# Mixing the values of batches 2 and 3 on two row halves of TensorE in four bursts, and a later place for one unit pair

## The chip, the cores and the metric

One core of one Trainium2 chip. The metric is the device time of a run in microseconds. The kernel before takes 250.5 us, so 2%, the limit of "faster", is 5 us.

## The reference, cut to what matters

```python
# attention: 4 batches, 8 heads, 768 positions, 64 per head; 8 blocks of 96
k_sorted = np.einsum('bhij,bhjcd->bhicd', P, k_b)      # P: 8x8 mixing matrix per head
v_sorted = np.einsum('bhij,bhjcd->bhicd', P, v_b)      # <- the changed part, for b = 2, 3
scores = scale * np.matmul(q_b, k_sb.transpose(0, 1, 2, 4, 3))
attn = softmax(scores)
x = np.matmul(attn, v_sb)                              # then to 3072 tokens x 512
# feed-forward
g = x @ w_gate; val = x @ w_val
out = (g / (1 + exp(-g)) * val) @ w_out
```

## The kernel before: the parts concerned

The feed-forward runs in eight passes of 384 tokens (`ffn(0)` to `ffn(7)`). A pass has twelve gate and twelve value groups of four matmuls and three output groups of twelve. Attention work for later passes is merged in between: each side item has a time, and is emitted after the first feed-forward item at whose end the running sum of costs has reached it. TensorE runs the items in the order emitted. A unit is the attention of two heads over four blocks of a batch: eight score matmuls, their exponentials, eight matmuls of probabilities and values, a normalisation on VectorE and, in this pass, four transposes. A burst is what the mixing emits at one place. Matmuls write to banks of PSUM, the memory that other engines then read or copy out.

```python
def v_pair_chunk(pair, at, n, eng, tag):        # mixes v of batches 2 and 3: all 128 rows
    dst = vt_tile(pair).rearrange("p u n e -> p (u n) e")
    mix = rmix["p"].rearrange("p u a b -> p (u a b)")      # 128 x 128, block diagonal
    tp = chunk_tile("tv", n // 4, tag).rearrange("p (l n) -> p l n", n=2 * H * NB)
    for ld in range(n):
        col = (at + ld) * C
        nc.tensor.matmul(tp[:, ld, :], lhsT=vch[:, col:col + 128], rhs=mix, start=True, stop=True)
    drain(eng, dst[:, :, at:at + n], tp[0:C].transpose([0, 2, 1]))   # copy out of PSUM
# ... cut ...
# gate -> tanh on ScalarE -> product gs on VectorE; value -> product h on VectorE.
# gate, value and (partly) output share three PSUM banks, tag "gen".
merge(ffn(1), ... + units(1, range(4), (11.3, 15.8)))
merge(ffn(3), vs(v_pair_chunk, 8, [1.15 * n for n in range(8)]) + units(2, range(4), (9.8, 14.0)))
```

Rows 0 to 63 of the values are batch 2, rows 64 to 127 batch 3, so half of the 128 x 128 mixing matrix is zeros. Mixing and scores share two double banks, tags "a" and "b".

The softmax here doesn't subtract the row's maximum and nothing guards it: scores larger than these inputs give would overflow.

Of the kernel before, what the change touches and what calls it, by code (L numbers as in the profile page):

```python
# [17 lines left out]
def kernel(  # L18
# [11 lines left out]
    nc = tc.nc  # L30

    B, H, S, D = q.shape
    NB = sort_net.shape[-1]
    C = S // NB
# [40 lines left out]
    vch = const.tile([128, D * C + 32], BF16)  # L75
# [51 lines left out]
    lowr, highr = slice(0, R), slice(R, 2 * R)  # L127
# [26 lines left out]
    rmix = {b: const.tile([128, 2, H, NB], BF16, name=f"rmix{b}") for b in (0, 1, "p")}  # L154
# [5 lines left out]
    def vt_tile(pair):  # L160
        if pair not in vts:
            t = vtp.tile([C, 2, H * NB, D + 1], BF16, name=f"vt{pair}", tag="vt")
            nc.vector.memset(t[:, :, :, D:D + 1].rearrange("p u n e -> p (u n) e"), 1.0)
            vts[pair] = t
        return vts[pair]
# [10 lines left out]
    def pair_tile(name, tag):  # L176
        return psum.tile([128, 1024], FP32, name=name, tag=tag)

    def bank_tile(name, tag="gen"):
        return psum.tile([128, 512], FP32, name=name, tag=tag, bufs=3 if tag == "gen" else 1)  # L180
# [28 lines left out]
    def drain(eng, dst, src):  # L209
        if eng == "v":  # L210
            nc.vector.tensor_copy(dst, src)  # L211
        else:
            nc.scalar.copy(dst, src)  # L213
# [10 lines left out]
    def chunk_tile(name, n, tag):  # L224
        return pair_tile(name, tag) if n == 2 else bank_tile(name, tag)
# [21 lines left out]
        drain(eng, dst[:, :, at:at + n], tp[0:C].transpose([0, 2, 1]))  # L247

    def v_pair_chunk(pair, at, n, eng, tag):
        dst = vt_tile(pair).rearrange("p u n e -> p (u n) e")  # L250
        mix = rmix["p"].rearrange("p u a b -> p (u a b)")
        tp = chunk_tile("tv", n // 4, tag).rearrange("p (l n) -> p l n", n=2 * H * NB)
        for ld in range(n):
            col = (at + ld) * C
            nc.tensor.matmul(tp[:, ld, :], lhsT=vch[:, col:col + 128], rhs=mix,  # L255
                             start=True, stop=True)
        drain(eng, dst[:, :, at:at + n], tp[0:C].transpose([0, 2, 1]))

    es, sts, xts = {}, {}, {}
    ecount = [0]  # L260
# [1 line left out]
    def scores(b, u, tag):  # L262
        half, g = divmod(u, H2)
        k_sb, k_at, q_sb, q_at = ((kqts[b], 0, kqts[b], GI * C) if b < 2 else
                                  (kqts["p"], (b - 2) * GI * C, kqts["q"], (b - 2) * GI * C))
        if tag == "gen":
            wide = None
            pss = [bank_tile("qk"), bank_tile("qk")]
        else:
            wide = pair_tile("qk", tag).rearrange("p (two n) -> p two n", two=2)  # L270
            pss = [wide[:, 0], wide[:, 1]]
        for i4 in range(4):
            at = (g * NB + half * 4 + i4) * C
            for two in range(2):
                lo = two * D
                nc.tensor.matmul(pss[two][:, i4 * C:(i4 + 1) * C],  # L276
                                 lhsT=k_sb[lo:lo + D, k_at + at:k_at + at + 128],
                                 rhs=q_sb[lo:lo + D, q_at + at:q_at + at + C],
                                 start=True, stop=True)
        return wide, pss  # L280

    def exps(b, u, wide, pss):
        n = ecount[0] % 8
        ecount[0] += 2
        if wide is None:
            for two in range(2):
                nc.scalar.activation(e_all[:, n + two, 0:4 * C], pss[two][0:C, 0:4 * C], AF.Exp, scale=scale)
        else:
            nc.scalar.activation(e_all[:, n:n + 2, 0:4 * C], wide[0:C, :, 0:4 * C], AF.Exp, scale=scale)  # L289
        es[(b, u)] = [e_all[:, n, :], e_all[:, n + 1, :]]  # L290

    def qk(b, u, tag="b"):
        exps(b, u, *scores(b, u, tag))
# [19 lines left out]
    def xt_tile(tag, n):  # L313
        bank = psum.tile([128, 1024], BF16, name="x_ps", tag=tag, bufs=3 if tag == "gen" else 1)
        return bank[:, 0:n * 4 * C].rearrange("p (g a b) -> p g a b", g=n, b=C)

    def x_to(dst, b, u):
        st = sts.pop((b, u))
        for i4 in range(4):
            nc.tensor.transpose(dst[:, i4, :], st[:, i4].rearrange("p a b -> p (a b)"),  # L320
                                ident[0:C, 0:C])

    def xtr(b, u):
        half, g = divmod(u, H2)
        if g == 0:
            xts[(b, half)] = xtp.tile([128, H2, TW], BF16, name=f"xt{b}_{half}", tag="xt")
        x_ps = xt_tile("x", 1)[:, 0]
        x_to(x_ps, b, u)
        return xts[(b, half)][:, g, :], x_ps.rearrange("p a b -> p (a b)")

    def x_dma(b, u):
        half, g = divmod(u, H2)
        if g == 0:
            xts[(b, half)] = xtp.tile([128, H2, TW], BF16, name=f"xt{b}_{half}", tag="xt")
        nc.sync.dma_start_transpose(out=xts[(b, half)][:, g, :].rearrange("p (i c) -> p i c", c=C),
                                    in_=sts.pop((b, u)).rearrange("p i two d -> p (i two d)"))
# [5 lines left out]
    def q_dma(b):  # L342
        dst = kqt_tile("q")[:, (b - 2) * GI * C:(b - 1) * GI * C]
        nc.sync.dma_start_transpose(out=dst.rearrange("p (g s) -> p g s", g=H2), in_=q_scr[b - 2])
# [5 lines left out]
    def gate(n, m):  # L350
        xt = xts[divmod(n, 2)]
        g_ps = psum.tile([128, TW], FP32, name="g_ps", tag="gen", bufs=3)
        for kc in range(NKC):
            nc.tensor.matmul(g_ps, lhsT=wg_sb[:, kc, ts(m, 128)], rhs=xt[:, kc, :],  # L354
                             start=(kc == 0), stop=(kc == NKC - 1))
        gate_out(n, m, g_ps)
# [66 lines left out]
    for it, n in ((1, 3), (2, 4), (3, 4), (4, 4)):  # L423
        nc.tensor.matmul(idle_ps[0:NB, 0:NB], lhsT=rowreds[it][:, :, 0], rhs=rowreds[it][:, :, 0],
                         start=True, stop=True)
# [38 lines left out]
    for b in range(1, B):  # L464
        rows = highr if b % 2 else lowr
# [49 lines left out]
    man = tc.manual_schedule(engines={ET.PE, ET.Pool})  # L515
    man.__enter__()

    def units(b, us, ats):
        us = list(us)
        todo = []  # L520
        for n, at in enumerate(ats):
            u, u2 = us[2 * n:2 * n + 2]
            held = []
            todo.append((at, lambda u=u, u2=u2, held=held: (qk(b, u, "b"), held.append(scores(b, u2, "a")))))
            todo.append((at + 1.3, lambda u2=u2, held=held: exps(b, u2, *held[0])))
            for w, tag, t in ((u, "b", 1.9), (u2, "a", 3.6)):
                if b == 0 or b == 1 and u < H2:
                    todo.append((at + t, lambda w=w, tag=tag: av(b, w, tag)))
                    todo.append((at + t + 3.1, lambda w=w: drain("v", *xtr(b, w))))
                else:  # L530
                    todo.append((at + t, lambda w=w, tag=tag: (av(b, w, tag), x_dma(b, w))))
        return todo

    def kqs(b, ats):
        return [(at, lambda n=n: (kq_chunk(b, n * 32, 16, "v", "b"), kq_chunk(b, n * 32 + 16, 16, "s", "a")))
                for n, at in enumerate(ats)]

    def vs(f, size, ats):
        return [(at, lambda m=m: f(1, m * size, size, "sv"[m % 2], "ba"[m % 2])) for m, at in enumerate(ats)]

    def merge(main, side):
        done, k = 0.0, 0
        side = sorted(side, key=lambda t: t[0])
        for c, f in main:
            f()
            done += c
            while k < len(side) and side[k][0] <= done:
                side[k][1]()
                k += 1
        while k < len(side):  # L550
            side[k][1]()
            k += 1

    def ffn(n):
        todo = []
        for m in range(NFC):
            if n > 0 or m > 1:
                todo.append((0.65, lambda m=m: gate(n, m)))
            if n > 0 or m > 0:
                todo.append((0.65, lambda m=m: value(n, m)))  # L560
            ends = (6, 9, 11) if n == 1 else (3, 7, 11)
            if n > 0 and m in ends:
                for part in range(3):
                    todo.append((0.87, lambda t3=ends.index(m), part=part: outp(n - 1, t3, part)))
        return todo
# [7 lines left out]
    q_cast(3)  # L573
    both = slice(0, 128)
    merge(ffn(0), units(0, range(4, 8), (0.0, 5.6)))
    merge(ffn(1), vs(v_chunk, 16, (3.2, 3.9, 4.7, 5.5)) + kqs(1, (6.2, 8.2, 10.3)) + units(1, range(4), (11.3, 15.8)))
    for s in range(4):
        copy_v(nc.gpsimd, 1, both, s)
    nc.vector.memset(kqt_tile("p")[:, 2 * GI * C:], 0.0)
    merge(ffn(2), units(1, range(4, 8), (0.0, 5.5)) + kqs("p", (13.0, 16.2, 19.4))  # L580
          + [(13.0, lambda: q_dma(2)), (16.4, lambda: q_dma(3))])
    merge(ffn(3), vs(v_pair_chunk, 8, [1.15 * n for n in range(8)]) + units(2, range(4), (9.8, 14.0)))
    merge(ffn(4), units(2, range(4, 8), (0.0, 8.0)))
    merge(ffn(5), units(3, range(4), (0.0, 8.0)))
    merge(ffn(6), units(3, range(4, 8), (0.0, 8.0)))
# [36 lines left out]
```

## Time and profile before

| | before |
|---|---|
| time, median (4 runs) | 250.51 us (249.94 to 250.79) |
| TensorE busy | 240.2 us, 97% of the span |
| VectorE, ScalarE busy | 157.4 us (63%), 110.3 us (44%) |
| TensorE's share of the chain that ends last | 88% |

The busy shares name TensorE, and the chain of waits confirms it. For a change this small the useful reading is finer: measure from start to start. I use the first scores near 62 us, those near 78 us, the first gate of the fourth pass near 107 us and the first scores of batch 2 near 121 us. In the timeline of TensorE before (columns: start, duration, group; in brackets, where there is one, the idle time before it and what ended that), the two of these that the prediction below does not show are:

```profile
62.20 0.52 PE L276 MATMUL qk<-kqt 64*128 64x96 bf16 x16
...
121.06 0.52 PE L276 MATMUL qk<-kqtq,kqtp 64*128 64x96 bf16 x16
```

So the second pass's stretch is 78.36 - 62.20 = 16.16 us (16.17 from the unrounded starts) and the fourth's is 121.06 - 107.00 = 14.06 us.

### The profile page before, as it was taken

The numbers are of one execution on the slowest core, as the hardware profiler recorded it, in microseconds if no ns is written. First come the engines' busy times: TensorE is split into PE (matmuls) and PEld (weight loads), VectorE is DVE, ScalarE is ACT, GpSimd is POOL, SyncE is SP. The second block draws the span as 40 slices with busy tenths as digits, with TensorE's granted clock in tenths as the row PEclk, the third lists the DMA queues.
The fourth block names the chain that finished last, engine by engine and source line by source line (L and its number), as shares of the span: only waits on it lengthen the run. The fifth ranks groups of instructions, "written<-read, shape, count | busy, mean of one in ns | idle before, by whom it ended". The sixth has DMA issues, their size and how long they took to land.

```text
span 248.1 us, 6062 instructions
## 1 busy us (share of the span) xinstructions
PE 240.2 (97%) x2572; PEld 142.9 (58%) x2572; DVE 157.4 (63%) x332; ACT 110.3 (44%) x187; POOL 52.6 (21%) x47
## 2 busy tenths in 40 slices
PE   7799999999999999999999999999999999999994
PEld 5385566665555556666655655555555555555543
DVE  6677689886555775857657647755764585446700
ACT  3977543453544444455642552354244334232311
POOL 7948449980039400000000000000000000000000
PEclk9999999999999999999999999999999999999999
DMA  5949999999999488010122121112111111100122
GB/s 97 215 83 162 208 198 223 190 219 222 219 175 188 74 195 179 3 42 3 42 53 56 52 67 32 44 45 74 36 42 42 40 55 55 45 19 24 45 81 88
DMA packets 39530, 24.38 MB, mean 98 GB/s; under 512 B 27728, under 2 KB 35664, under 8 KB 38992
## 3 DMA queue, kind: packets, MB, share of 16 engines
q0 software_dynamic: 21328, 14.16, 39.0%
q1 hardware_dynamic: 18176, 9.84, 14.3%
q8 instruction: 20, 0.33, 0.5%
q14 instruction: 6, 0.05, 0.1%
HBM read 28.32 MB, written 7.86 MB: 146 GB/s over the span
## 4 chain that ended last, share of the span: by engine, by line
PE 88%; DVE 4%; ACT 3%; issue 2%; DMA 2%; DVEq 0%; ACTq 0%; POOLq 0%
PE v_ps L372 24%; PE g_ps L354 23%; PE o_ps L389 23%; PE tkq L233 4%; PE av_ps L303 3%; PE qk L276 3%; DMA v<-in_v_dram 2%; PE idle_ps L415 2%; PE tv L245 2%; PE tv L255 1%; DVE gs_sb L364 1%; PE o_ps L405 1%; DVE st L309 1%; PE x_ps L320 1%; DVE h L377 1%
## 5 line engine op out<-in xcount | busy, mean ns | idle before, releaser
L364 DVE SCALAR_TENSOR_TENSOR gs_sb<-th_sb,g_ps 128x384 bf16<-128x384 bf16 x96 | 52.8, 550 | 53.8 <-ACT th_sb L362 51.2
L372 PE MATMUL v_ps<-xt,wv_sb 128*128 128x384 bf16 x380 | 77.3, 326 | 0.3
L354 PE MATMUL g_ps<-xt,wg_sb 128*128 128x384 bf16 x376 | 76.5, 325 | 0.0
L362 ACT ACTIVATE th_sb<-g_ps 128x384 bf16<-128x384 f32 x96 | 47.1, 491 | 57.6 <-PE g_ps L354 55.2
L389 PE MATMUL o_ps<-wo_sb,h 128*128 128x512 bf16 x276 | 64.3, 379 | 0.0
L377 DVE SCALAR_TENSOR_TENSOR h<-v_ps,gs_sb 128x384 bf16<-128x384 f32 x96 | 53.3, 555 | 6.4
L372 PEld LDWEIGHTS <-wv_sb 128*128 128x128 bf16 x380 | 35.6, 97 | 23.9 <-issue 1.2
L354 PEld LDWEIGHTS <-wg_sb 128*128 128x128 bf16 x376 | 34.5, 97 | 22.9 <-issue 0.2
L389 PEld LDWEIGHTS <-h 128*128 128x128 bf16 x276 | 26.3, 98 | 28.3
L394 ACT COPY o_sb<-o_ps 128x512 f32<-128x512 f32 x23 | 13.5, 586 | 49.1 <-PE o_ps L389 46.4
L124 POOL COPY vch<-v 64x1536 bf16<-64x1536 bf16 (+2 forms) x11 | 28.8, 2648 | 20.6 <-PE av_ps L303 17.2
L289 ACT ACTIVATE e_all<-qk 96x768 bf16<-96x768 f32 x30 | 22.6, 802 | 7.7 <-PE qk L276 7.6
L309 DVE TENSOR_TENSOR st<-av_ps,r_sb 96x512 bf16<-96x512 f32 x32 | 21.7, 679 | 0.2
L303 PEld LDWEIGHTS <-e_all 96*128 96x128 bf16 x256 | 12.2, 98 | 5.0 <-ACT e_all L289 0.8
L303 PE MATMUL av_ps<-vt,e_all 96*128 96x65 bf16 x256 | 13.5, 194 | 0.0
L307 DVE RECIPROCAL r_sb<-av_ps 96x8 f32<-96x8 f32 x32 | 6.4, 199 | 8.7 <-PE av_ps L303 8.6
L213 ACT CAST vt<-tv 96x1024 bf16<-96x1024 f32 (+1 forms) x9 | 9.2, 1030 | 4.0 <-PE tv L255 2.6
L211 DVE CAST vt<-tv 96x1024 bf16<-96x1024 f32 (+1 forms) x9 | 9.8, 1100 | 1.2 <-PE tv L245 1.2
L211 DVE CAST kqt<-tkq 128x1024 bf16<-128x1024 f32 (+1 forms) x7 | 7.4, 1068 | 2.5 <-PE tkq L233 2.4
L213 ACT CAST kqt<-tkq 128x1024 bf16<-128x1024 f32 (+1 forms) x7 | 6.0, 894 | 6.4 <-PE tkq L233 6.4
L415 PE MATMUL idle_ps<-warm_sb 128*128 128x512 bf16 x28 | 8.3, 388 | 0.0
L233 PE MATMUL tkq<-rmix,kq 128*64 128x64 bf16 x384 | 7.8, 197 | 0.4 <-issue 0.4
(74 smaller groups left out, 130.5 us busy)
## 6 DMA issues: line engine op xcount, KB each, us to landing
out_dram<-o_sb SPq DMA_DIRECT2D x23, 256.0 KB, 2.0
v<-in_v_dram POOLq DMA_DIRECT2D x3, 768.0 KB, 19.7
kq<-in_q_dram POOLq DMA_DIRECT2D x2, 768.0 KB, 14.1
wg_sb<-in_moe_w_gate_dram POOLq DMA_DIRECT2D x6, 256.0 KB, 9.4
wv_sb<-in_moe_w_val_dram POOLq DMA_DIRECT2D x6, 256.0 KB, 9.8
wo_sb<-in_moe_w_out_dram POOLq DMA_DIRECT2D x1, 1536.0 KB, 24.5
kp<-in_k_dram POOLq DMA_DIRECT2D x2, 768.0 KB, 15.1
q_scr<-in_q_dram POOLq DMA_DIRECT2D x2, 768.0 KB, 30.0
```

Source lines behind the costliest of these rows:

```text
L124: eng.tensor_copy(dst, src.transpose([0, 2, 1]))
L211: nc.vector.tensor_copy(dst, src)
L233: nc.tensor.matmul(tp[two * D:(two + 1) * D, lc, :], lhsT=kq_tiles[b][:, at + lc, :], rhs=rm[:, two], start=True, stop=True)
L289: nc.scalar.activation(e_all[:, n:n + 2, 0:4 * C], wide[0:C, :, 0:4 * C], AF.Exp, scale=scale)
L303: nc.tensor.matmul(o[:, two, i4, :], lhsT=e[:, i4 * C:i4 * C + 128], rhs=vt[:, 2 * g + two, half * 4 + i4, :], start=True, stop=True)
L309: nc.vector.tensor_tensor(st.rearrange("p i two d -> p two i d"), o[0:C, :, :, 0:D], r_sb.to_broadcast([C, 2, 4, D]), op=ALU.mult)
L354: nc.tensor.matmul(g_ps, lhsT=wg_sb[:, kc, ts(m, 128)], rhs=xt[:, kc, :], start=(kc == 0), stop=(kc == NKC - 1))
L362: nc.scalar.activation(th_sb, g_ps, AF.Tanh, scale=0.5)
L364: nc.vector.scalar_tensor_tensor(gs_sb, th_sb, 1.0, g_ps, op0=ALU.add, op1=ALU.mult)
L372: nc.tensor.matmul(v_ps, lhsT=wv_sb[:, kc, ts(m, 128)], rhs=xt[:, kc, :], start=(kc == 0), stop=(kc == NKC - 1))
L377: nc.vector.scalar_tensor_tensor(h_tiles[n][:, m, :], v_ps, 0.5, gs_tiles.pop(m), op0=ALU.mult, op1=ALU.mult)
L389: nc.tensor.matmul(o_ps, lhsT=h_w[:, m, ts(t3, 128)], rhs=wo_sb[:, m, :], start=(m == 0), stop=(m == NFC - 1))
```

## The change

The intent: a 64-row matmul needs only half of TensorE's rows, so the two batches can be mixed side by side, each with 64 columns in place of 128 that are half zeros. The pairs come in four bursts in place of eight, each with one copy for VectorE and one for ScalarE. Separately, the second unit pair of the second pass is put 0.6 further in.

```diff
     def v_pair_chunk(pair, at, n, eng, tag):
-        dst = vt_tile(pair).rearrange("p u n e -> p (u n) e")
-        mix = rmix["p"].rearrange("p u a b -> p (u a b)")
-        tp = chunk_tile("tv", n // 4, tag).rearrange("p (l n) -> p l n", n=2 * H * NB)
+        dst = vt_tile(pair)[:, :, :, at:at + n]
+        tp = chunk_tile("tv", n // 4, tag).rearrange("p (u l n) -> p u l n", u=2, n=H * NB)
         for ld in range(n):
             col = (at + ld) * C
-            nc.tensor.matmul(tp[:, ld, :], lhsT=vch[:, col:col + 128], rhs=mix,
-                             start=True, stop=True)
-        drain(eng, dst[:, :, at:at + n], tp[0:C].transpose([0, 2, 1]))
+            for u, rows in enumerate((lowr, highr)):
+                nc.tensor.matmul(tp[:, u, ld, :], lhsT=vch[rows, col:col + 128],
+                                 rhs=rmix["p"][rows, u].rearrange("p a b -> p (a b)"),
+                                 start=True, stop=True)
+        drain(eng, dst, tp[0:C].transpose([0, 1, 3, 2]))
 # ... cut: units() takes a lag per unit pair, 3.1 where it was fixed ...
+    def v_pairs(ats):
+        return [(at, lambda m=m: (v_pair_chunk(1, m * 16, 8, "v", "b"), v_pair_chunk(1, m * 16 + 8, 8, "s", "a")))
+                for m, at in enumerate(ats)]
 # ... cut ...
-    merge(ffn(1), ... + units(1, range(4), (11.3, 15.8)))
+    merge(ffn(1), ... + units(1, range(4), (11.3, 16.4), (3.1, 2.5)))
-    merge(ffn(3), vs(v_pair_chunk, 8, [1.15 * n for n in range(8)]) + units(2, range(4), (9.8, 14.0)))
+    merge(ffn(3), v_pairs([2.6 * n for n in range(4)]) + units(2, range(4), (9.8, 14.0)))
```

More of the change, by code (lines that the diff above doesn't have):

```diff
@@ L516, with units @@
     man.__enter__()
-    def units(b, us, ats):
+    def units(b, us, ats, lags=(3.1, 3.1)):
         us = list(us)
@@ L522, in units @@
             u, u2 = us[2 * n:2 * n + 2]
+            lag = lags[n]
             held = []
@@ L528, in units @@
                     todo.append((at + t, lambda w=w, tag=tag: av(b, w, tag)))
-                    todo.append((at + t + 3.1, lambda w=w: drain("v", *xtr(b, w))))
+                    todo.append((at + t + lag, lambda w=w: drain("v", *xtr(b, w))))
                 else:
@@ L575 @@
     merge(ffn(0), units(0, range(4, 8), (0.0, 5.6)))
-    merge(ffn(1), vs(v_chunk, 16, (3.2, 3.9, 4.7, 5.5)) + kqs(1, (6.2, 8.2, 10.3)) + units(1, range(4), (11.3, 15.8)))
+    merge(ffn(1), vs(v_chunk, 16, (3.2, 3.9, 4.7, 5.5)) + kqs(1, (6.2, 8.2, 10.3))
+          + units(1, range(4), (11.3, 16.4), (3.1, 2.5)))
     for s in range(4):
```

## The prediction

> **What bounds the kernel now.** I read the page first, then the list of waits, then the timeline of TensorE around the changed code, then those of VectorE and ScalarE in the same stretch. The page's busy line, its TensorE slices and its chain:
>
> ```profile
> PE 240.2 (97%) x2572; PEld 142.9 (58%) x2572; DVE 157.4 (63%) x332; ACT 110.3 (44%) x187; POOL 52.6 (21%) x47
> PE   7799999999999999999999999999999999999994
> PE 88%; DVE 4%; ACT 3%; issue 2%; DMA 2%; DVEq 0%; ACTq 0%; POOLq 0%
> ```
>
> TensorE is full in all slices but the first two and the last, and holds 88% of the chain that ends last. So time saved on TensorE between 24 and 240 us should reach the end one for one, and time that another engine costs counts only where TensorE must wait for it. The list of waits says how much of that there is:
>
> ```profile
> ACT th_sb L362 <- PE g_ps L354: 55.2, 62, 1.3
> DVE gs_sb L364 <- ACT th_sb L362: 51.2, 31, 2.8
> ...
> PE qk L276 <- DVE st L309: 0.6, 1, 0.6
> ```
>
> The long waits are all of other engines for TensorE. After the start, TensorE has one recorded wait of its own: 0.6 us, once. Now the code of the change. The timeline of TensorE, columns start, duration, group:
>
> ```profile
> 107.00 0.81 PE L354 MATMUL g_ps<-xt,wg_sb 128*128 128x384 bf16 x4
> 107.65 0.61 PE L255 MATMUL tv<-rmixp,vch 128*128 128x128 bf16 x8
> 108.10 0.81 PE L372 MATMUL v_ps<-xt,wv_sb 128*128 128x384 bf16 x4
> 108.75 0.61 PE L255 MATMUL tv<-rmixp,vch 128*128 128x128 bf16 x8
> 109.19 0.81 PE L354 MATMUL g_ps<-xt,wg_sb 128*128 128x384 bf16 x4
> ```
>
> From start to start a gate or value group of four takes 0.65 us and a mixing burst of eight takes 0.445 us, 55.6 ns a matmul. Nothing waits; all eight bursts, up to 118.57, go like this. The second place, in the second pass:
>
> ```profile
> 67.32 1.03 PE L389 MATMUL o_ps<-wo_sb,h 128*128 128x512 bf16 x4
> 68.28 0.34 PE L276 MATMUL qk<-kqt 64*128 64x96 bf16 x8
> 69.20 0.34 PE L276 MATMUL qk<-kqt 64*128 64x96 bf16 x8 [0.58 <-DVE st L309]
> 69.48 0.34 PE L320 MATMUL x_ps<-ident,st 96*128 96x96 bf16 x4
> 69.66 1.89 PE L389 MATMUL o_ps<-wo_sb,h 128*128 128x512 bf16 x8
> ...
> 77.62 0.81 PE L354 MATMUL g_ps<-xt,wg_sb 128*128 128x384 bf16 x4
> 78.36 0.51 PE L276 MATMUL qk<-kqt 64*128 64x96 bf16 x16
> 78.81 0.82 PE L372 MATMUL v_ps<-xt,wv_sb 128*128 128x384 bf16 x4
> ```
>
> Here is the 0.58 us wait: the scores of the fourth unit need a bank pair that VectorE still normalises from. The last three rows are my only sample of matmuls on two row halves among full ones: 16 of them, eight pairs.
>
> **What the Trainium skill says.** "TensorE: Matmul & The Clock Gate", Part 3, The mechanism: matmuls in different row groups run at the same time, starts some 4 ns apart. The trace agrees: a score matmul lasts 203 to 213 ns, and the 16 end 0.51 us after the first start, so seven pair steps take some 0.30 us, 43 ns a pair. The same page, Part 1, "Wait — 56ns, not 53.3ns?": a warm matmul starts every N/2.4 + 2.5 ns. For N = 96 that is 42.5 ns, for N = 128 55.8 ns, both as seen; for N = 64 it is 29.2 ns, and the unpaired 64-column mixing of batch 1 goes at 0.46/16 = 29 ns here. "TensorEngine Tiling (Array Packing)", Key Properties: changing the tiling mode drains TensorE. The trace shows it: gate start to score start is 0.74 instead of 0.65 us, and the eight pairs, 0.34 us of steps, take 0.45 us until the next group starts. A visit to row halves costs 0.09 us to enter and 0.11 us to leave. Its section PSUM Bottleneck: tiling doesn't speed the copies out of PSUM, which may then bind. This is my main doubt.
>
> **Part 1, the mixing.** It removes 64 matmuls of 128 columns and adds 64 pairs of 64 columns; the two halves of a pair go to different banks, as the scores do. Bursts become four, of 16 pairs (two copies' worth) each.
> Before: 8 x 0.445 = 3.56 us. After, per burst: 0.09 + 16 x 0.0292 + 0.11 = 0.67 us, four are 2.68 us. Gross: -0.88 us. Of the 1.87 us that pairing halves away, the mode changes eat 0.8, plus rounding; fewer, longer bursts are what makes pairing pay at all.
>
> Now the copies. They stay eight of 1024 columns, four on each engine, but come two at once:
>
> ```profile
> 112.72 0.56 DVE L364 SCALAR_TENSOR_TENSOR gs_sb<-th_sb,g_ps 128x384 bf16<-128x384 bf16 x1 [0.88 <-ACT th_sb L362]
> 113.19 1.22 DVE L211 CAST vt<-tv 96x1024 bf16<-96x1024 f32 x1
> 114.32 0.54 DVE L377 SCALAR_TENSOR_TENSOR h<-v_ps,gs_sb 128x384 bf16<-128x384 f32 x1
> ```
>
> VectorE starts a gate or value product 0.47 us after the one before (0.65 us if it needs that one's result), and 1.13 us after a copy; ScalarE's copies last 1.18 us. Gate and value share three banks, so the value of chunk m+1 reuses the bank of gate m, and must wait until that gate's tanh and product are done. I worked the new order through by hand with these durations and a lag of 0.20 us from TensorE's next start to the reader's start; the same working with the old order gives the traced starts to 0.1 us and no wait. Times from the first gate of this pass (107.00 before):
> - Burst 1 from 0.65 to 1.32; gate 1 and value 1 end at 3.27; burst 2 to 3.94. VectorE is through value product 1 at 4.57 and starts its copy of burst 2; ScalarE starts its own at 4.06.
> - Gate 2 ends at 4.59. Its tanh could start at 4.8 but follows the copy, 5.13; its product follows both, 5.70, and frees the bank at 6.25. Value 3 would start at 5.90: TensorE waits 0.4 us. Before, this place had nothing to spare either (free at 6.28, wanted at 6.33).
> - After burst 4 the output copy and then the second copy hold ScalarE until 12.1, so gate 4's tanh is late, its product frees the bank at 13.17, and value 5 wants it at 12.87: 0.3 us. Before, the eighth burst lay between gate 4 and value 4 and covered this.
> Together 0.7 us if the lags are right. The chain of three lags is good to about 0.15 us at each place, and a shorter ScalarE copy would take 0.1 us off the second, so I count 0.6 us: net -0.28 us.
>
> **Part 2, the second unit pair.** The build of both kernels shows that the scores stay after the same output group: only the four transposes (69.48, 0.18 us) move ahead of them, and the two later value products with their transposes move back by one group. The wait ends when VectorE ends, at 69.20, whatever came before; so the transposes fill 0.18 us of it, and some 0.4 us of wait stay. Later, VectorE copies the last two transposes in a row and late; by my working the last one may wait 0.04 us. Net: -0.15 us.
>
> **Sum.** 250.35 - 0.28 - 0.15 = 249.92, say **249.9 us**.
>
> **Rivals.**
> - Pairing at full worth with no new wait (the copies hide): -0.88 - 0.15, 249.3 us. For it: the key-mixing bursts at 97.45 and 101.97 also feed both copies at once and stall nothing. Against: those last 1.1 us, so VectorE has more time per copy; and here three such bursts fall in 5.9 us of work.
> - The halves don't overlap (bank or weight-load limits): 128 x 29.2 ns + 0.8 = 4.5 us, +1.0 us, with fewer stalls 251.1 us. Against: the scores, same shapes of weights, do overlap.
> - VectorE and ScalarE become the bound of the stretch, stalls of over 1 us: 250.3 us or a little more. For it: between bursts 1 and 2 VectorE needs 1.13 + 4 x 0.5 = 3.1 us of TensorE's 3.27. Against: the outputs after burst 3 need no VectorE and let it catch up.
>
> **Range and chances.** The three runs of before spread 0.85 us, so the median of the new ones has some 0.3 us of noise; the cases above reach from 249.3 to 250.3 for what I believe possible. Range 249.2 to 250.5. The 2% limit is 5 us, more than all mixing matmuls together cost: within 2% 0.98, each side 0.01.
>
> **What would show it.** Right: 128 mixing matmuls of about 190 ns in four bursts, 0.67 us from burst start to next start; two new TensorE waits on VectorE's gate product, 0.2 to 0.5 us each, in the fourth pass before value 3 and value 5; the wait of the scores near 69 us cut to some 0.4 us with the transposes before it; the rest merely shifted. Wrong: a burst of over 0.9 us (no overlap), no waits in the fourth pass (then nearer 249.3), or a new wait near 76 us before the last transposes.

## The result, and the profile after

The changed kernel takes 249.74 us (median of 4 runs, 249.61 to 250.03) against 250.51 us. Ratios here are the mean time of one kernel's fast runs over that of the other's of the same rounds, so not quite the ratio of these medians: 0.9974, with a 95% interval of 0.9952 to 0.9995. 249.74 lies 0.2 us from the predicted 249.9.

The page of the changed kernel, its busy line and its chain:

```profile
PE 240.1 (97%) x2636; PEld 141.3 (57%) x2636; DVE 157.7 (64%) x332; ACT 110.3 (44%) x187; POOL 52.5 (21%) x47
...
PE 83%; DVE 7%; ACT 3%; issue 3%; DMA 2%; DVEq 0%; ACTq 0%; POOLq 0%
```

TensorE is as busy as before, 64 matmul records more, but its share of the chain is 5 points lower, and VectorE's 3 points higher. TensorE's own waits in the list (total us, times, longest), after 62 us:

```profile
PE qk L277 <- DVE st L310: 0.4, 1, 0.4
PE v_ps L373 <- DVE gs_sb L365: 0.4, 2, 0.2
```

The old wait is shorter, and there is a new kind: value matmuls that wait for VectorE's product of a gate. (The changed file is longer, so L373 is L372 of before, L365 is L364, and so on.) The timeline of TensorE in the fourth pass:

```profile
107.06 0.81 PE L355 MATMUL g_ps<-xt,wg_sb 128*128 128x384 bf16 x4
107.81 0.64 PE L255 MATMUL tv<-rmixp,vch 64*128 64x64 bf16 x32
108.38 0.82 PE L373 MATMUL v_ps<-xt,wv_sb 128*128 128x384 bf16 x4
...
112.32 0.81 PE L355 MATMUL g_ps<-xt,wg_sb 128*128 128x384 bf16 x4
113.35 0.81 PE L373 MATMUL v_ps<-xt,wv_sb 128*128 128x384 bf16 x4 [0.21 <-DVE gs_sb L365]
...
119.25 0.81 PE L355 MATMUL g_ps<-xt,wg_sb 128*128 128x384 bf16 x4
120.23 0.81 PE L373 MATMUL v_ps<-xt,wv_sb 128*128 128x384 bf16 x4 [0.17 <-DVE gs_sb L365]
120.97 0.51 PE L277 MATMUL qk<-kqtq,kqtp 64*128 64x96 bf16 x16
```

A burst of 16 pairs takes 108.38 - 107.06 - 0.65 = 0.67 us, modes included. Mind the numbers in brackets: a matmul's shown end overlaps its successor (0.81 us shown for a group that starts the next one after 0.65), so 0.21 us of listed idle time is 113.35 - 112.32 - 0.65 = 0.38 us of lost time, and 0.17 is 0.33. Measure from start to start. The pass takes 120.97 - 107.06 = 13.91 us, 0.15 less than before.

What holds the gate product is seen in the timelines of ScalarE and VectorE there:

```profile
111.12 1.19 ACT L213 CAST vt<-tv 96x1024 bf16<-96x1024 f32 x1 [0.74 <-PE tv L255]
112.18 0.49 ACT L363 ACTIVATE th_sb<-g_ps 128x384 bf16<-128x384 f32 x1
...
111.63 1.22 DVE L211 CAST vt<-tv 96x1024 bf16<-96x1024 f32 x1
112.76 0.54 DVE L365 SCALAR_TENSOR_TENSOR gs_sb<-th_sb,g_ps 128x384 bf16<-128x384 bf16 x1
...
117.47 0.58 ACT L395 COPY o_sb<-o_ps 128x512 f32<-128x512 f32 x1 [1.51 <-PE o_ps L390]
118.04 1.18 ACT L213 CAST vt<-tv 96x1024 bf16<-96x1024 f32 x1
119.11 0.48 ACT L363 ACTIVATE th_sb<-g_ps 128x384 bf16<-128x384 f32 x1
...
119.62 0.55 DVE L365 SCALAR_TENSOR_TENSOR gs_sb<-th_sb,g_ps 128x384 bf16<-128x384 bf16 x1 [0.59 <-ACT th_sb L363]
```

Both engines copy a burst just when gate 2 ends (at 111.67); tanh and product follow their copy, and value 3 needs the bank that they free. Before value 5 it is ScalarE alone that is late: it copies an output and then the burst, gate 4 has ended at 118.59 but its tanh starts at 119.11, and VectorE, done with its own copy, stands idle for 0.59 us until the tanh is there. The second place of the change:

```profile
68.38 0.34 PE L321 MATMUL x_ps<-ident,st 96*128 96x96 bf16 x4
68.65 0.34 PE L277 MATMUL qk<-kqt 64*128 64x96 bf16 x8
69.39 0.34 PE L277 MATMUL qk<-kqt 64*128 64x96 bf16 x8 [0.41 <-DVE st L310]
69.67 1.90 PE L390 MATMUL o_ps<-wo_sb,h 128*128 128x512 bf16 x8
```

The transposes now fill 0.17 us of the wait. The whole stretch from 62 to 78 us takes 16.04 us, 0.13 less than before.

So the traces show 0.15 + 0.13 = 0.28 us of gain (0.26 with what the unchanged stretches differ by), a third of the difference of the first medians.

### The profile page after: what moved, and what is told of

It is laid out like the page before. It is cut to its first block, busy times and chain, and to the rows that moved or that the text cites. A ratio compares the mean times of both kernels' runs of the same rounds, so it can differ in the third digit from the quotient of the medians.

```text
span 248.0 us, 6193 instructions
## 1 busy us (share of the span) xinstructions
PE 240.1 (97%) x2636; PEld 141.3 (57%) x2636; DVE 157.7 (64%) x332; ACT 110.3 (44%) x187; POOL 52.5 (21%) x47
## 4 chain that ended last, share of the span: by engine, by line
PE 83%; DVE 7%; ACT 3%; issue 3%; DMA 2%; DVEq 0%; ACTq 0%; POOLq 0%
PE v_ps L373 23%; PE o_ps L390 23%; PE g_ps L355 22%; PE tkq L233 4%; PE av_ps L304 3%; PE qk L277 2%; DVE gs_sb L365 2%; DMA v<-in_v_dram 2%; DVE st L310 2%; PE tv L245 2%; PE idle_ps L416 1%; DVE h L378 1%; PE o_ps L406 1%; ACT th_sb L363 1%; PE x_ps L321 1%
## 5 line engine op out<-in xcount | busy, mean ns | idle before, releaser
L365 DVE SCALAR_TENSOR_TENSOR gs_sb<-th_sb,g_ps 128x384 bf16<-128x384 bf16 x96 | 52.8, 550 | 51.8 <-ACT th_sb L363 49.1
L373 PE MATMUL v_ps<-xt,wv_sb 128*128 128x384 bf16 x380 | 77.3, 326 | 0.7 <-DVE gs_sb L365 0.4
L373 PEld LDWEIGHTS <-wv_sb 128*128 128x128 bf16 x380 | 35.4, 97 | 24.6 <-issue 2.3
```

The source lines that it names most:

```text
L365: nc.vector.scalar_tensor_tensor(gs_sb, th_sb, 1.0, g_ps, op0=ALU.add, op1=ALU.mult)
L373: nc.tensor.matmul(v_ps, lhsT=wv_sb[:, kc, ts(m, 128)], rhs=xt[:, kc, :], start=(kc == 0), stop=(kc == NKC - 1))
```

## The experiments

All eight runs gave a correct output. "Before" was timed again on the same chip. This table holds the stretches of each profile, from start to start of the same matmuls, in us:

| run | start to 62 | 62 to 78 | 78 to 107 | 107 to 121 | 121 to end |
|---|---|---|---|---|---|
| before | 62.20 | 16.17 | 28.64 | 14.06 | 127.01 |
| after | 62.38 | 16.04 | 28.64 | 13.91 | 127.03 |
| x4_again | 63.90 | 16.03 | 28.64 | 13.91 | 127.02 |
| x1_units_only | 62.84 | 16.04 | 28.64 | 14.06 | 127.02 |
| x2_pairs_only | 64.01 | 16.17 | 28.64 | 13.91 | 127.00 |
| x3_spread | 62.88 | 16.03 | 28.64 | 13.21 | 127.00 |
| x5_bursts_full_rows | 61.96 | 16.03 | 28.64 | 14.94 | 127.03 |
| x6_pairs_eight | 62.07 | 16.03 | 28.64 | 14.06 | 127.02 |
| x7_scores_later | 64.09 | 15.46 | 28.64 | 13.91 | 127.01 |
| x8_both | 61.93 | 15.46 | 28.64 | 13.21 | 127.01 |

My theory: pairs overlap fully; of their gain the mode changes and two new waits leave 0.15 us, the unit shift brings as much, and nothing else changes. Rivals: one part brings all of the 0.65 to 0.77 us; or the pairs are held by something other than these waits.

**x4_again**: no edit.

> The changed kernel once more, unaltered, for a tighter ratio. In its first trace the stretch from the first gate of the fourth pass to the scores of batch 2 took 13.91 us against 14.06 before, and the stretch from the output group at 67 us to the scores at 78 us 10.91 against 11.04: 0.3 us in all. If the two parts are everything, the times differ by 0.3 us (ratio 0.9988); if the 0.65 to 0.77 us of the first timing are real, something outside these stretches gained as well (ratio 0.997).

Median 249.81 us against 250.16 us; ratio 0.9978, interval 0.9945 to 1.0011. All stretches after 62 us repeat to 0.01 us, but this profile's span is 1.5 us longer than the first one's, all of it before 62 us, where no instruction was changed. TensorE's waits between 22 and 62 us in this profile (total, times, longest):

```profile
PE qk L277 <- issue: 1.1, 1, 1.1
PE v_ps L373 <- DMA wv_sb<-in_moe_w_val_dram: 0.6, 1, 0.6
```

Once it stood still for a reason that the profile doesn't show ("issue"), once it waited for value weights on their way from memory. The same list is empty for the first two profiles. Such waits early in the run come and go between runs, and move the time by more than the change does; x1_units_only, x2_pairs_only, x3_spread and x7_scores_later each have one or more for weights there. These five profiles reach 62 us at 62.84 to 64.09; the other five, with no listed wait of TensorE between 22 and 62 us, at 61.93 to 62.38. The repeated ratio is no tighter than the first; both intervals hold the traces' 0.26 us (0.9990).

**x1_units_only**: the kernel before with the unit shift alone.

```diff
# ... cut: units() takes a lag per unit pair, as in the change ...
-    merge(ffn(1), ... + units(1, range(4), (11.3, 15.8)))
+    merge(ffn(1), ... + units(1, range(4), (11.3, 16.4), (3.1, 2.5)))
```

> Only the shift of the second unit pair, mixing as before. My theory: the stretch at 67 to 78 us takes 10.9 us instead of 11.04, the fourth pass 14.06 as before, time 0.15 us less than before. Rival: the shift is what brought the measured gain, 0.5 us or more.

16.04 and 14.06 us, as expected of my theory. The time, 249.84 us, ratio 0.9987 (0.9955 to 1.002), can't tell 0.13 us from nothing; the stretch can.

**x2_pairs_only**: the changed kernel with the unit pair back at 15.8.

```diff
-    merge(ffn(1), ... + units(1, range(4), (11.3, 16.4), (3.1, 2.5)))
+    merge(ffn(1), ... + units(1, range(4), (11.3, 15.8)))
```

> Only the mixing in pairs and bursts, units as before. My theory: the fourth pass takes 13.9 us, with the two TensorE waits on gate products before value 3 and value 5; the stretch at 67 us stays 11.04; time 0.15 us less than before. Rival: the pairs bring the whole measured gain, 0.5 us or more.

16.17 and 13.91 us, with both waits on the gate product. Time 249.99 us, ratio 0.9996 (0.9961 to 1.0032). The parts are independent and worth 0.13 and 0.15 us; after 62 us neither holds a hidden half microsecond.

**x3_spread**: the bursts elsewhere.

```diff
-    merge(ffn(3), v_pairs([2.6 * n for n in range(4)]) + units(2, range(4), (9.8, 14.0)))
+    merge(ffn(3), v_pairs((1.9, 3.8, 6.9, 8.4)) + units(2, range(4), (9.8, 14.0)))
```

> The changed kernel with its four bursts after gate 1, value 2, the second part of the output group and gate 4, instead of after gate 0, value 1, value 3 and the output group. My theory: copies of a burst no longer meet the late gates, the two waits vanish, and the fourth pass takes 13.2 us (14.06 - 0.88), 0.7 us less than in the changed kernel; time 0.7 us less than it, about 1.0 less than before. Rival (the waits are only shown, and the time of the stretch is set by the copying engines anyway): the waits turn up in other places and the pass stays near 13.9 us.

13.21 us. The timeline has every group of the pass at its pace, the gate and value after a burst too:

```profile
112.23 0.64 PE L255 MATMUL tv<-rmixp,vch 64*128 64x64 bf16 x32
112.80 0.82 PE L355 MATMUL g_ps<-xt,wg_sb 128*128 128x384 bf16 x4
113.47 0.81 PE L373 MATMUL v_ps<-xt,wv_sb 128*128 128x384 bf16 x4
```

Gate 3 to value 3 is 0.67 us where it was 1.03. The waits are gone, so they, and not the copying engines' rate, cost the 0.70 us; the pairs themselves are worth 14.06 - 13.21 = 0.85 us, close to the 0.88 worked out. Median 248.80 us, ratio 0.9947 (0.9916 to 0.9978); about 0.9960 would follow from the stretches (0.99 us of 250), and the interval holds it.

**x5_bursts_full_rows**: the changed kernel with the mixing function of before, in four bursts.

```diff
# ... cut: dst, mix, tp and the copy as before the change ...
-            for u, rows in enumerate((lowr, highr)):
-                nc.tensor.matmul(tp[:, u, ld, :], lhsT=vch[rows, col:col + 128], ...)
+            nc.tensor.matmul(tp[:, ld, :], lhsT=vch[:, col:col + 128], rhs=mix, start=True, stop=True)
```

> The changed kernel with the mixing matmuls of before (128 columns, all rows) in the four bursts. A burst then takes 16 x 55.6 ns = 0.89 us. My theory (the two waits come from two copies starting together just ahead of a gate, however fast the matmuls were): the waits before value 3 and value 5 stay, some 0.45 us each from start to start, and the fourth pass takes about 14.9 to 15.0 us, 0.9 more than before. Rival (the waits come from the pairs being faster than the copies): no waits, 14.06 us as before.

14.94 us; 251.08 us, ratio 1.0026 (0.9978 to 1.0075). In its timeline value 3 starts late with bursts of 0.89 us, too:

```profile
112.32 0.81 PE L354 MATMUL g_ps<-xt,wg_sb 128*128 128x384 bf16 x4
113.41 0.81 PE L372 MATMUL v_ps<-xt,wv_sb 128*128 128x384 bf16 x4 [0.28 <-DVE gs_sb L364]
```

113.41 - 112.32 - 0.65 = 0.44 us, and as much before value 5. So the waits belong to the four bursts, not to the speed of the pairs. Bursting alone costs 0.88 us.

**x6_pairs_eight**: the changed kernel with its pairs in the eight places of before.

```diff
-    merge(ffn(3), v_pairs([2.6 * n for n in range(4)]) + units(2, range(4), (9.8, 14.0)))
+    merge(ffn(3), vs(v_pair_chunk, 8, [1.15 * n for n in range(8)]) + units(2, range(4), (9.8, 14.0)))
```

> The changed kernel with its pairs in the eight places of before, eight pairs a visit. My theory: a visit costs 8 x 29 ns and 0.21 us for changing to row halves and back, 0.44 us, as much as the full-row burst of before; no waits; the fourth pass takes 14.05 us, as before. Rival (changing costs less when it happens often, or pairing is worth more): 13.0 to 13.5 us.

14.06 us and no wait, 250.09 us, ratio 0.9988 (0.9945 to 1.003). Three lines of its timeline show the price of a visit:

```profile
106.74 0.81 PE L355 MATMUL g_ps<-xt,wg_sb 128*128 128x384 bf16 x4
107.48 0.41 PE L255 MATMUL tv<-rmixp,vch 64*128 64x64 bf16 x16
107.82 0.82 PE L373 MATMUL v_ps<-xt,wv_sb 128*128 128x384 bf16 x4
```

107.82 - 106.74 - 0.65 = 0.43 us for eight pairs whose own steps take 8 x 29 = 233 ns. The rest, 0.2 us, is as much as in a burst of 16 pairs (0.67 - 16 x 0.029 = 0.2 us): a price of the visit to row halves, not of the pairs. Pairing alone, in the old places, is worth nothing.

**x7_scores_later**: the unit pair one real step further.

```diff
-    merge(ffn(1), ... + units(1, range(4), (11.3, 16.4), (3.1, 2.5)))
+    merge(ffn(1), ... + units(1, range(4), (11.3, 16.5), (3.1, 2.4)))
```

> The changed kernel with the second unit pair of the second pass at 16.5 instead of 16.4, which moves its scores behind one more part of the output group; lag 2.4 instead of 2.5, so that the transposes stay where they are. My theory: the wait for VectorE's normalisation, 0.59 us from start to start in the changed kernel, goes entirely, as VectorE is done before; the stretch from the scores at 62 us to those at 78 takes 15.5 us instead of 16.04. Rival: the later scores push the exponentials and with them the probabilities-times-values matmuls, which wait instead: 15.9 us or more.

15.46 us, 0.58 less than the changed kernel, and the list of waits has no wait of the scores for VectorE any more. The sum of costs passes 15.61, 16.48 and 17.35 here, so 15.8 and 16.4 both fall on 16.48, and only 16.5 reaches the next place. Time 250.10 us with four runs from 248.90 to 251.15, ratio 0.9979 (0.9931 to 1.0027): inconclusive alone; its profile reached the scores at 62 us 1.7 us later than the changed kernel's first one.

**x8_both**: the edits of x3_spread and x7_scores_later.

> The spread bursts of x3_spread and the later scores of x7_scores_later together. If both are single waits on TensorE's path they add: fourth pass 13.2 us, stretch from 62 to 78 us 15.5 us, 1.5 us less than before in all, 248.7 us, ratio 0.994. If either is taken back later, the stretch after the scores at 121 us grows beyond its 127.0 us.

13.21 and 15.46 us, and 127.01 at the end: they add, (14.06 - 13.21) + (16.17 - 15.46) = 1.56 us. Median 248.81 us against 250.31 us; ratio 0.9938 (0.99 to 0.9976), which is what 1.56 of 250 us gives. This version beats both kernels, the changed one by 0.70 + 0.58 = 1.3 us by the stretches.

## Why the prediction was right, point by point

- **The bound.** TensorE's time does reach the end one for one: in every run the stretches add, and those that were not touched repeat within 0.03 us. What the reading of before missed is the part ahead of 62 us, which I took as fixed at its profiled length; in ten profiles it lies between 61.93 and 64.09 us.
- **Pairs overlap.** 128 matmuls of 190 ns; in the trace the two of a pair start 3 to 4 ns apart and pairs follow every 29 ns, as worked out. The rival without overlap (+1.0 us gross) is ruled out by this.
- **Mode changes.** Worked out as 0.67 us a burst, measured 0.67 us. x6_pairs_eight shows the price by itself.
- **The copies' collision.** The working put gate 2's tanh at 5.13 us of the pass, its product at 5.70 and value 3 at 6.30; the trace has 5.12, 5.70 and 6.29. For value 5 it had some 13.2, the trace 13.17. It had the two causes right as well: both engines' copies ahead of value 3, ScalarE's two copies in a row ahead of value 5. x3_spread and x5_bursts_full_rows show that the four bursts' places bring the waits; which copy holds which product is read from the timelines. The skill's page "TensorEngine Tiling (Array Packing)", PSUM Bottleneck, warns of the copies and advises using both engines for them; that was done here, and it was the place of the copies, just ahead of a gate, that stopped TensorE. The rival that has the copies bind the stretch falls with x3_spread, the rival of full worth and no wait with the trace itself.
- **Where a size was off.** Part 1 was put at -0.28 us and measured -0.15 us. The step is "so I count 0.6 us": the working gave 0.7 us of waits, and 0.38 + 0.33 = 0.71 us came. The 0.1 us was taken off for a shorter ScalarE copy, but the four copies took 1.18 to 1.20 us, no less than before. That makes 0.11 of the 0.13 us; the rest is the gross gain, 0.85 us by x3_spread, worked out as 0.88.
- **Two slips that did not enter the sum.** Pairing takes away 3.56 - 1.87 = 1.69 us; 1.87 us is what the 64 pairs still cost (1.69 less 0.8 gives the 0.88 of the working, but for rounding). And the third rival's 3.27 us is not the time between bursts 1 and 2: the trace has 110.44 - 107.81 = 2.63 us from one to the next, in which VectorE does one copy and three products, 2.72 us from copy to copy (108.91 to 111.63). So VectorE does fall a little behind there.
- **Part 2.** Put at -0.15, measured -0.13 us: 0.17 us of wait filled, and the small wait before the last transposes, foreseen as 0.04 us, is in the trace with 0.04 us (76.64 - 74.87 us from the output group's start to the transposes, against 76.58 - 74.85 before).
- **The sum.** -0.43 us predicted, -0.26 us by the traces. The medians' -0.77 us and -0.35 us scatter around it; that 249.74 lies so near 249.9 owes something to luck, as the runs of one kernel spread over 2 us. What makes the early waits come and go is not settled by these runs.

## What to carry to other kernels

Halving the columns of small matmuls by pairing row halves worked at full worth here, but each visit to row halves had a fixed price of 0.2 us, so count visits before counting matmuls, and make visits long. Longer visits bring their copies in a lump: check which product or activation queues behind the lump and which bank it holds, because there a full TensorE can stop; moving the bursts by one to three places gave 0.70 of the 0.71 us back here. Where the time's noise exceeds the effect, compare start-to-start stretches between fixed events of the traces, and look whether a changed schedule constant moves an item at all.

## What the Trainium skill lacked or had wrong

- "TensorEngine Tiling (Array Packing)", Key Properties, says that changing the tiling mode drains TensorE, but not what it costs: here some 0.2 us a visit to row halves and back (0.67 us for 16 pairs of 29 ns; 0.43 us for 8).
- "TensorE: Matmul & The Clock Gate", Part 3, gives measured speedups of packing for 512 columns; for two row halves with 64 columns each the runs show a pair every 29 ns, so full doubling, with loads of 128 weight columns between them.
- "Trainium Kernel Development and Optimization", Performance Expectations ("Reading a trace"), says that matmul busy time is a bad metric because matmuls are pipelined. It lacks the counterpart: listed waits come out short by the same overlap (0.21 us listed, 0.38 us lost).
- No page that I read has the spread of a run's first part by weights that land late and by a stop without a recorded cause: 61.93 to 64.09 us to the same instruction in ten profiles, with listed waits in the five of 62.84 us and more and none in the other five.
